# Attention decode with FFN on one core: scores on TensorE over K transposed on chip, softmax of four items in rows, one load queue

## The chip, the cores and the metric

One core of one Trainium2 chip. The metric is the device time of one execution, in microseconds (us), the median of several runs. All runs told here are fast ones. "Span" is the time from the first to the last instruction in the profiled run; in every run that lists both, the device time is 1.7 to 2.2 us longer.

The engines in the profile: PE is TensorE (PEld its weight loads), DVE is VectorE, ACT is ScalarE, POOL is GpSimd, SP is the sync engine that issues loads. A name with q (POOLq, SPq) is that engine's sequencer. L743 is line 743 of the kernel profiled.

## The reference

```
# x [2,1,640]; 32 heads, head size 192; the last 2048 of 8192 cached rows are used; bf16
h  = x + attention(layernorm(x)) @ wo       # softmax(q k^T / sqrt(192)) v, for each of 32 heads x 2 batches
h2 = h + (gelu(n @ w_gate) * (n @ w_up)) @ w_down          # n = layernorm(h), F = 1536
```

One query row per batch against 64 (head, batch) pairs, called items here. Each item has its own K and V of 2048 x 192, 768 KB each: 100.7 of the 122.3 MB that must be read.

## The kernel before

Items lie with 2048 = 128 partitions x 16 rows. VectorE makes the scores, 16 multiply-and-reduce instructions per item against a q row broadcast to all partitions (5 of the 64 items go through TensorE instead). The softmax needs a max and a sum over all partitions; GpSimd makes them for a pair of items at a time:

```python
KS = 4; VS = 4                       # buffers of K and of V
...
def armaxG(gi):                                        # GpSimd
    W(g, sem_v_max, gi + 1)
    ins = g.partition_all_reduce(mb_[:, a0:a0 + k], m1[:, a0:a0 + k], channels=128, reduce_op=RMAX)
    W(g, sem_g_chain, sem_g_chain.inc(ins))
    ins = g.tensor_scalar(out=nm[:, a0:a0 + k], in0=mb_[:, a0:a0 + k], scalar1=-1.0, scalar2=None, op0=ALU.mult)
    assert sem_g_nm.inc(ins) == gi + 1
def arsumG(gi):
    W(g, sem_a_exp, grp[-1] + 1)
    ins = g.partition_all_reduce(zb[:, a0:a0 + k], rs[:, a0:a0 + k], channels=128, reduce_op=RADD)
...
def ttr(n):                                            # VectorE, scores of item n
    for t in range(T):                                 # T = 16
        ins = v.tensor_tensor_reduce(out=junk[:, di % 2, t, :], in0=kring[:, slot, t * DH:(t + 1) * DH],
                                     in1=qb_ring[:, di % QBR, :], ..., accum_out=s_all[:, n, t:t + 1])
...
def expo(m):                                           # ScalarE
    W(a, sem_g_nm, GIDX[m] + 1)
    ins = a.activation(out=e_ring[:, m % ER, :, _row(b)], in_=s_all[:, m, :], func=ACT.Exp,
                       bias=nm[:, m:m + 1], scale=1.0, accum_out=rs[:, m:m + 1])
def pv(m):                                             # TensorE: 16 matmuls of 192 columns per item
    ...
# SP: V of item n is loaded when pv(n - 4) is done, K when the scores of the item 4 before are done
```

Of the kernel before, what the change touches and what calls it, by code (L numbers as in the profile page):

```python
# [7 lines left out]
I32 = mybir.dt.int32  # L8
# [3 lines left out]
RMAX = bass.bass_isa.ReduceOp.max  # L12
RADD = bass.bass_isa.ReduceOp.add

B = 2
D = 640
HQ = 32
# [4 lines left out]
F = 1536  # L22
NIT = B * HQ
EPS = 1e-5
# [3 lines left out]
KS = 4  # L28
VS = 4
WQR = 3  # L30
WOR = 4
QBR = 8
ER = 4
NWQ = 8
NGROUP = 16
R1 = 32
NCH = 3
QB_OFF = 256
SC_OFF = 448
QT_OFF = 464  # L40
OFF_HEADS = (11, 23, 35, 47, 59)


class _Sem:
    def __init__(self, sem):
        self.sem = sem
        self.count = 0

    def inc(self, ins, n=1):
        ins.then_inc(self.sem, n)  # L50
        self.count += n
        return self.count


def _row(b):
    return 0 if b == 0 else R1


def bass_sequential_preLN__sliding_block_cached__geglu_ffn__decode_kernel(
# [11 lines left out]
):  # L71
    with ExitStack() as ctx:  # L72
# [6 lines left out]
        def sb(shape, dt):  # L79
            return ctx.enter_context(nc.sbuf_tensor(_nm("sb"), shape, dt))  # L80

        def ps(shape, dt):
            return ctx.enter_context(nc.psum_tensor(_nm("ps"), shape, dt))

        def S(name):
            return _Sem(ctx.enter_context(nc.semaphore(name)))

        kring = sb([128, KS, T * DH], BF16)
        vring = sb([128, VS, T * DH], BF16)
        wqring = sb([128, WQR, 5, 768], BF16)  # L90
        woring = sb([128, WOR, 3, D], BF16)
        wg_sb = sb([128, 5, F], BF16)
        wu_sb = sb([128, 5, F], BF16)
        wd_sb = sb([128, 12, D], BF16)
        s_all = sb([128, NIT, T], F32)
        junk = sb([128, 2, T, DH], BF16)
        e_flat = sb([128, ER * T * 33 // 2], I32)
        e_ring = e_flat[:, :].bitcast(BF16).rearrange("p (a b c) -> p a b c", a=ER, b=T)
        qb_ring = sb([128, QBR, DH], BF16)
        xbc = sb([128, 2, 5, 128], BF16)  # L100
        koff = sb([128, T * DH], BF16)
        kta_sb = sb([128, 2, 8, 128], BF16)
        ktb_sb = sb([128, 2, 8, 128], BF16)
        qt_sb = sb([128, 2, 2], BF16)
        m1 = sb([128, NIT], F32)
        mb_ = sb([128, NIT], F32)
        nm = sb([128, NIT], F32)
        rs = sb([128, NIT], F32)
        zb = sb([128, NIT], F32)
        rinv = sb([128, NIT], F32)  # L110
        o_sb = sb([128, 2, 384], BF16)
        ot_flat = sb([128, 48 * 33 // 2], I32)
        ot_ext = ot_flat[:, :].bitcast(BF16).rearrange("p (a b) -> p a b", a=48)
        iota_i = sb([128, 128], I32)
        lib_scr = sb([128, 2], F32)
        burn_rhs = sb([128, 512], BF16)
        ident = sb([128, 128], BF16)
        selb = sb([128, 2, 128], BF16)
        xin = sb([128, D], BF16)
        x33f = sb([128, D], F32)  # L120
        stats = sb([128, 2, 6], F32)
        mv = sb([128, 2], F32)
        rstd = sb([128, 1], F32)
        sd1 = sb([128, 1], F32)
        sd2 = sb([128, 1], F32)
        dum = sb([1, 8], F32)
        eps_t = sb([128, 1], F32)
        xn_bf = sb([128, D], BF16)
        h_sb = sb([128, D], F32)
        stats2 = sb([128, 2, 6], F32)  # L130
        mv2 = sb([128, 2], F32)
        rstd2 = sb([128, 1], F32)
        hn_bf = sb([128, D], BF16)
        hT_ext = sb([128, 5, 33], BF16)
        g_bf = sb([128, F], BF16)
        u_bf = sb([128, F], BF16)
        fA = sb([128, F], BF16)
        fB = sb([128, F], BF16)
        fC = sb([128, F], BF16)
        uT_flat = sb([128, 12 * 33 // 2], I32)  # L140
        uT_ext = uT_flat[:, :].bitcast(BF16).rearrange("p (a b) -> p a b", a=12)
        h2_bf = sb([128, D], BF16)

        h_ps_a = ps([128, 512], F32)
        h_ps_b = ps([128, 512], F32)
        o_ps = [ps([128, 512], F32) for _ in range(2)]
        t_ps = [ps([128, 512], F32) for _ in range(2)]
        x_ps = [ps([128, 512], F32) for _ in range(2)]

        semK = [S(f"semK{i}") for i in range(KS)]  # L150
        semV = [S(f"semV{i}") for i in range(VS)]
        semWQ = [S(f"semWQ{i}") for i in range(WQR)]
        semWO = [S(f"semWO{i}") for i in range(WOR)]
        sem_x = S("sem_x")
        semKoff = S("semKoff")
        sem_wg = S("sem_wg")
        sem_wu = S("sem_wu")
        sem_wd = S("sem_wd")
        sem_out = S("sem_out")
        sem_v_ttr = S("v_ttr")  # L160
        sem_v_max = S("v_max")
        sem_v_rcp = S("v_rcp")
        sem_v_misc = S("v_misc")
        sem_v_chain = S("v_chain")
        sem_v_mv = S("v_mv")
        sem_v_init = S("v_init")
        sem_v_xbc = S("v_xbc")
        sem_v_hT = S("v_hT")
        sem_v_in = S("v_in")
        sem_v_pr = S("v_pr")  # L170
        sem_g_nm = S("g_nm")
        sem_g_z = S("g_z")
        sem_g_misc = S("g_misc")
        sem_g_chain = S("g_chain")
        sem_a_exp = S("a_exp")
        sem_a_oev = S("a_oev")
        sem_a_qb = S("a_qb")
        sem_a_kt = S("a_kt")
        sem_a_qt = S("a_qt")
        sem_a_sc = S("a_sc")  # L180
        sem_a_otev = S("a_otev")
        sem_a_misc = S("a_misc")
        sem_a_sd = S("a_sd")
        sem_a_xbc = S("a_xbc")
        sem_a_x1 = S("a_x1")
        sem_a_gev = S("a_gev")
        sem_a_uev = S("a_uev")
        sem_a_sg = S("a_sg")
        sem_a_ut = S("a_ut")
        sem_p_pv = S("p_pv")  # L190
        sem_p_qb = S("p_qb")
        sem_p_kt = S("p_kt")
        sem_p_qt = S("p_qt")
        sem_p_sc = S("p_sc")
        sem_p_tr = S("p_tr")
        sem_p_op = S("p_op")
        sem_p_misc = S("p_misc")
        sem_p_chain = S("p_chain")
        sem_p_gu = S("p_gu")
        sem_p_ut = S("p_ut")  # L200

        block = ctx.enter_context(nc.Block())

        def W(eng, sem, val):
            if val > 0:
                eng.wait_ge(sem.sem, val)
# [5 lines left out]
        def wq_src(J, c):  # L212
            return A_wq[128 * c:128 * (c + 1), 768 * J:768 * (J + 1)]

        def wo_src(g):
            return A_wo[384 * g:384 * (g + 1), :].rearrange("(p kk) n -> p kk n", kk=3)

        def wq_wait_val(J):
            slot, use = J % WQR, J // WQR
            if slot == 0:  # L220
                return 16 + 80 * use
            return 80 * (use + 1)

        def qb_bank_idx(m):
            if m < 9:
                return 1
            G = (m - 8) // 4
            return (G + 1) % 2

        def qb_bank(m):  # L230
            return t_ps[qb_bank_idx(m)]

        AUX = {}

        def _add_aux(n, fn):
            AUX.setdefault(n, []).append(fn)

        def _mk_wq(J, c):
            def fn(eng):
                if J >= WQR and c == 0:  # L240
                    last_m = 8 * (J - WQR) + 7
                    while last_m in OFF_IDX:
                        last_m -= 1
                    W(eng, sem_p_qb, DV_IDX[last_m] + 1)
                semWQ[J % WQR].inc(eng.dma_start(wqring[:, J % WQR, c, :], wq_src(J, c)), 16)  # L245
            return fn

        for _J in range(1, NWQ):
            for _c in range(5):
                _add_aux([0, 0, 1, 1, 2][_c] if _J == 1 else 8 * _J - 10 + _c, _mk_wq(_J, _c))  # L250

        def _mk_wo(gq):
            def fn(eng):
                if gq >= WOR:
                    W(eng, sem_p_op, gq - WOR + 1)
                semWO[gq % WOR].inc(eng.dma_start(woring[:, gq % WOR, :, :], wo_src(gq)), 16)
            return fn

        for _gq in range(NGROUP):
            _add_aux(4 * _gq + 2, _mk_wo(_gq))  # L260

        GROUPS = [[2 * P, 2 * P + 1] for P in range(NIT // 2 - 1)] + [[NIT - 2], [NIT - 1]]
        GIDX = {}
        for gi, grp in enumerate(GROUPS):
            for m in grp:
                GIDX[m] = gi
        RMAX_AT = {grp[-1] + 1: gi for gi, grp in enumerate(GROUPS)}
        RCP_AT = {grp[-1] + 2: gi for gi, grp in enumerate(GROUPS)}
# [23 lines left out]
        def k_slot(m):  # L292
            return DV_IDX[m] % KS
# [569 lines left out]
```

## Time and profile before

| | before |
|---|---|
| time at the prediction, three runs | 690.6 us (686.4 to 692.8) |
| span, mean TensorE clock granted | 685.9 us, 0.648 |
| bytes read, mean rate | 122.3 MB, 178 GB/s |
| busy: TensorE, VectorE, ScalarE, GpSimd | 42%, 42%, 15%, 5% |

The page is read from its head: busy shares first (is an engine full?), then the rate of the loads in 40 slices, then the waits, then the chain that ended last. The prediction below shows these lines and reads them; one reading of GpSimd in it is mended further down.

### The profile page before, as it was taken

The page shows a single profiled execution, that of the slowest core. Times are in us where ns is not written, and L with a number is a line of the kernel's source. Part 1 is how long each engine was busy: PE and PEld are TensorE (multiplying, and loading weights), DVE is VectorE, ACT ScalarE, POOL GpSimd, SP SyncE. Part 2 cuts the span into 40 slices and gives each one's busy share as a digit, 9 for nine tenths or more (in the row PEclk, how much of TensorE's full clock was granted, in tenths as well). Part 3 has the DMA queues.
Part 4 walks back from the last instruction along what each step waited for, and adds up shares of the span by engine and source line. Part 5 has one row for each costly group of instructions (what it writes and reads, how often), then busy time and mean ns, then how long its engine had stood idle before and what let it go on. Part 6 is the DMA issues. An engine that isn't in the chain of part 4 may idle for free.

```text
span 685.9 us, 7188 instructions
## 1 busy us (share of the span) xinstructions
PE 286.3 (42%) x1936; PEld 198.9 (29%) x1936; DVE 289.2 (42%) x2003; ACT 102.4 (15%) x328; POOL 37.0 (5%) x107
## 2 busy tenths in 40 slices
PE   3135643312783331277433118534421853333247
PEld 1024532201452221145222115423320542222123
DVE  4752344355344425533433555443245554332214
ACT  2112210110221101022101113111101311110013
POOL 1000000000000000000000000000000000000100
PEclk9556556766556666655567666666665656665659
DMA  8764525546542555545355455445644444548000
GB/s 328 280 224 169 182 97 201 217 176 231 207 179 103 183 216 184 211 184 190 106 200 226 167 198 207 179 154 186 242 148 168 184 167 184 200 160 318 0 0 1
DMA packets 28351, 122.76 MB, mean 179 GB/s; under 512 B 3092, under 2 KB 8216, under 8 KB 28312
## 3 DMA queue, kind: packets, MB, share of 16 engines
q1 hardware_dynamic: 20248, 103.63, 40.0%
q10 hardware_dynamic: 8064, 18.68, 8.3%
q8 instruction: 16, 0.26, 0.1%
q14 instruction: 23, 0.19, 0.1%
HBM read 122.29 MB, written 0.00 MB: 178 GB/s over the span
## 4 chain that ended last, share of the span: by engine, by line
issue 66%; DVE 15%; PE 9%; POOL 5%; ACT 2%; POOLq 1%; ACTq 1%; DVEq 0%
DVE sb L446 14%; PE ps L743 4%; POOL sb L333 2%; POOL sb L343 2%; ACT sb L553 1%; POOL sb L335 1%; PE ps L639 1%; PE ps L714 1%; PE ps L713 1%; POOLq L72 1%; ACTq L245 1%; DVE sb L434 1%; DVE sb L427 1%; PE ps L813 0%; PE ps L816 0%
## 5 line engine op out<-in xcount | busy, mean ns | idle before, releaser
L743 PE MATMUL ps<-sb 128*33 128x192 bf16 (+1 forms) x1024 | 156.2, 339 | 361.8 <-ACT sb L553 352.3
L446 DVE CUSTOM_DVE_ANT_0 sb<-sb 128x192 bf16<-128x192 bf16 x944 | 268.5, 352 | 16.0 <-issue 15.4
L743 PEld LDWEIGHTS ps<-sb 128*33 128x33 bf16 (+1 forms) x1024 | 119.8, 125 | 399.1 <-ACT sb L553 371.5
L434 DVE RECIPROCAL sb<-sb 128x2 f32<-128x2 f32 (+1 forms) x33 | 5.5, 166 | 359.1 <-POOL sb L343 359.1
L446 DVE DVE_READ_ACCUMULATOR2_ANT sb<- 128x1 f32 x944 | 76.9, 82 | 0.0
L553 ACT ACTIVATE sb<-sb 128x16 bf16<-128x16 f32 x64 | 21.1, 356 | 314.5 <-POOL sb L335 314.5
L680 PE MATMUL ps<-sb 128*128 128x192 bf16 x295 | 40.5, 277 | 17.7 <-ACT sb L535 11.5
L521 ACT ACTIVATE sb<-ps 128x192 bf16<-128x192 f32 x59 | 19.5, 331 | 156.2 <-PE ps L680 155.8
L680 PEld LDWEIGHTS ps<-sb 128*128 128x128 bf16 x295 | 25.1, 107 | 27.9 <-issue 27.0
L565 ACT ACTIVATE sb<-ps,sb 1x192 bf16<-1x192 f32 x64 | 26.2, 410 | 30.2 <-DVE sb L434 29.3
L343 POOL PARTITION_ALL_REDUCE sb<-sb x33 | 13.4, 405 | 214.7 <-issue 214.7
L335 POOL TENSOR_SCALAR sb<-sb 128x2 f32<-128x2 f32 (+1 forms) x33 | 8.3, 252 | 261.2 <-issue 261.2
L714 PE MATMUL ps<-sb 128*64 128x128 bf16 x80 | 22.3, 279 | 0.0
L713 PE MATMUL ps<-sb 128*128 128x128 bf16 x80 | 20.7, 258 | 0.0
L333 POOL PARTITION_ALL_REDUCE sb<-sb x33 | 13.0, 394 | 132.3 <-DVE sb L427 132.3
L770 PE MATMUL ps<-sb 128*33 128x512 bf16 x48 | 19.0, 467 | 0.5 <-ACT sb L571 0.5
L528 ACT ACTIVATE sb<-ps 128x1024 bf16<-128x1024 bf16 x10 | 10.2, 1024 | 52.2 <-PE ps L714 52.2
L726 PE MATMUL ps<-sb 128*128 128x1 bf16 x80 | 14.3, 179 | 0.4 <-ACT sb L521 0.4
L728 PE MATMUL ps<-sb 64*128 64x1 bf16 x80 | 14.1, 176 | 0.0
L772 PE MATMUL ps<-sb 128*33 128x128 bf16 x48 | 12.0, 250 | 0.0
L553 ACT ACTIVATION_READ_ACCUMULATOR sb<-sb 128x1 f32 x64 | 11.9, 186 | 0.0
L714 PEld LDWEIGHTS ps<-sb 128*64 128x64 bf16 x80 | 9.3, 117 | 7.8 <-issue 0.8
(84 smaller groups left out, 134.9 us busy)
## 6 DMA issues: line engine op xcount, KB each, us to landing
sb<-in_A_v_cache_dram SPq DMA_DIRECT2D x64, 768.0 KB, 5.4
sb<-in_A_k_cache_dram SPq DMA_DIRECT2D x59, 768.0 KB, 5.8
sb<-in_A_wo_dram ACTq DMA_DIRECT2D x16, 480.0 KB, 3.6
sb<-in_A_wq_dram ACTq DMA_DIRECT2D x35, 192.0 KB, 2.8
sb<-in_A_k_cache_dram ACTq DMA_DIRECT2D x5, 768.0 KB, 4.4
sb<-in_B_w_gate_dram SPq DMA_DIRECT2D x5, 384.0 KB, 8.3
sb<-in_B_w_up_dram SPq DMA_DIRECT2D x5, 384.0 KB, 8.4
sb<-in_B_w_down_dram SPq DMA_DIRECT2D x3, 640.0 KB, 11.4
```

The source lines that it names most:

```text
L333: ins = g.partition_all_reduce(mb_[:, a0:a0 + k], m1[:, a0:a0 + k], channels=128, reduce_op=RMAX)
L335: ins = g.tensor_scalar(out=nm[:, a0:a0 + k], in0=mb_[:, a0:a0 + k], scalar1=-1.0, scalar2=None, op0=ALU.mult)
L343: ins = g.partition_all_reduce(zb[:, a0:a0 + k], rs[:, a0:a0 + k], channels=128, reduce_op=RADD)
L446: ins = v.tensor_tensor_reduce(out=junk[:, di % 2, t, :], in0=kring[:, slot, t * DH:(t + 1) * DH], in1=qb_ring[:, di % QBR, :], scale=1.0, ...
L521: ins = a.activation(out=qb_ring[:, di % QBR, :], in_=qb_bank(m)[:, QB_OFF:QB_OFF + DH], func=ACT.Copy, scale=SCALE)
L553: ins = a.activation(out=e_ring[:, m % ER, :, _row(b)], in_=s_all[:, m, :], func=ACT.Exp, bias=nm[:, m:m + 1], scale=1.0, accum_out=rs[:, ...
L565: ins = a.activation(out=o_sb[r:r + 1, G % 2, (h % 2) * DH:(h % 2 + 1) * DH], in_=o_ps[m % 2][r:r + 1, 0:DH], func=ACT.Copy, scale=rinv[r: ...
L680: ins = pe.matmul(t_ps[bank][:, QB_OFF:QB_OFF + DH], lhsT=xbc[:, b, c, :], rhs=wqring[:, J % WQR, c, hoff:hoff + DH], start=(c == 0), stop ...
L713: pe.transpose(xa_view[:, 128 * tt:128 * (tt + 1)], koff[:, t * DH:t * DH + 128], ident[:, :])
L714: ins = pe.transpose(xb_view[0:64, 128 * tt:128 * (tt + 1)], koff[:, t * DH + 128:(t + 1) * DH], ident[:, :])
L743: ins = pe.matmul(o_ps[m % 2][0:M, 0:DH], lhsT=e_ring[:, m % ER, t, 0:M], rhs=vring[:, m % VS, t * DH:(t + 1) * DH], start=(t == 0), stop= ...
L770: pe.matmul(h_ps_a[0:33, :], lhsT=ot_ext[:, k, 0:33], rhs=woring[:, gq % WOR, kk, 0:512], start=first, stop=last)
```

## The change

Its intent is to take the work that sits on partitions away from VectorE and GpSimd. K is transposed on TensorE, 24 transposes of 128x128 per item, and copied back to SBUF by VectorE and ScalarE. Scores then are matmuls with four items in four groups of 32 PSUM partitions (four column tiles of the array). An item's softmax lies in 4 rows of 512 columns, so the max and the sum over columns are ordinary reductions, and the combination of the 4 rows is a small matmul with a mask. The output, h, the norms and the FFN are kept transposed. GpSimd only fills constants. All loads go on SP's queue, with 6 K and 8 V buffers. The waits come from a small list of dependences rather than by hand.

```diff
-KS = 4
-VS = 4
...
+KS = 6
+VS = 8
+KTS = 8
...
-                ins = g.partition_all_reduce(mb_[:, a0:a0 + k], m1[:, a0:a0 + k], channels=128, reduce_op=RMAX)
...
-                    ins = v.tensor_tensor_reduce(
...
+                        for jj in range(8):                      # transposes(n), for c in range(3)
+                            off = 384 * jj + 128 * c
+                            ins = e.transpose(bv[:, 128 * jj:128 * (jj + 1)], kring[:, slot, off:off + 128],
+                                              identb[:, :])
...
+                if c == 2 or (c == 1 and n % 4 == 1):
+                    act(lambda e, ...: e.activation(out=ktr[:, kslot, c, :], in_=bv[:, 0:1024], func=ACT.Copy), ...)
+                else:
+                    dve(lambda e, ...: e.tensor_copy(ktr[:, kslot, c, :], bv[:, 0:1024]), ...)
...
+                for k in range(6):                               # scores(g)
+                    for j in range(4):
+                        ins = e.matmul(sps[32 * j:32 * (j + 1), :], lhsT=rq[:, g % 2, j, k, :], rhs=r, start=(k == 0),
+                                       stop=(k == 5), tile_position=(0, 32 * j))
+            dve(lambda e: e.tensor_reduce(out=mx[:, :], in_=sps[:, :], axis=AX.X, op=ALU.max), W=["mx"], X=["s"])
...
+            pe(lambda e: e.matmul(m2[:, 0:4], lhsT=pm[:, :], rhs=mrhs[:, :], start=True, stop=True), ...)
...
+                    for cc in range(4):                          # pv(g), per item
+                        for r in range(4):
+                            ins = e.matmul(ops_[32 * r:32 * (r + 1), 192 * hh:192 * (hh + 1)],
+                                           lhsT=ering[:, g % 2, col:col + 32], rhs=vring[:, n % VS, DH * t:DH * (t + 1)],
+                                           ..., tile_position=(0, 32 * r), skip_group_check=True)
...
```

(The rest, some 1,400 lines of it, is the same idea for q, o, the norms and the FFN.)

## The prediction

> **What bounds the kernel now.** I read the head of the page first: no engine is near full (TensorE 42%, VectorE 42%), and the DMA rate starts at 328 GB/s, then stays mostly between 100 and 240.
>
> ```profile
> PE 286.3 (42%) x1936; PEld 198.9 (29%) x1936; DVE 289.2 (42%) x2003; ACT 102.4 (15%) x328; POOL 37.0 (5%) x107
> GB/s 328 280 224 169 182 97 201 217 176 231 207 179 103 183 216 184 211 184 190 106 200 226 167 198 207 179 154 186 242 148 168 184 167 184 200 160 318 0 0 1
> ```
>
> So nothing is short of throughput; something is a chain. The waits by total, with the DMA queue's own, say which (engine, line, what it waited for: us in total, times, longest):
>
> ```profile
> DVE sb L434 <- POOL sb L343: 359.1, 33, 14.6
> ACT sb L553 <- POOL sb L335: 314.5, 33, 15.1
> POOL sb L335 <- issue: 261.2, 33, 11.3
> POOL sb L343 <- issue: 214.7, 33, 7.2
> ...
> SPq L361 <- PE ps L743: 463.3, 59, 18.1
> ```
>
> Each occurs 33 times, once per pair of (head, batch) items. L333 and L343 are GpSimd's max and sum over partitions; the "issue" after them is GpSimd's real time in them. SPq L361 is the queue's V load, held 463 us in all until a PV (L743) frees its buffer. One round of the chain that ended last, in order of time (start, us, what), shows the order:
>
> ```profile
> 87.82 0.39 POOL sb L333
> 88.21 0.06 POOLq L335 x2
> 88.28 7.00 issue
> 95.27 0.26 POOL sb L335
> ...
> 96.06 0.20 ACT sb L553
> 96.25 5.46 issue
> 101.71 0.42 POOL sb L343
> 102.13 0.02 issue
> 102.15 0.17 DVE sb L434
> ```
>
> 7.5 us of max, a negation, the exp, some 6 us of sum, reciprocal: serial on GpSimd, with a part of VectorE's scores between. L333 starts 33 times between 25.2 and 649.0 us: (649.0-25.2)/32 = 19.5 us a round, 33 rounds = 643 of the 686 us. The bound is **GpSimd's cross-partition softmax round**, through PV to the V buffers. The DMA could do far more, as the table of stretches shows (from:to, length, busy time of each engine, clock, DMA share, GB/s):
>
> ```profile
> 8.00:14.00 6.00, 4.06 (x18) 1.62 (x18) 4.16 (x11) 0.50 (x3) 1.50 (x2) 1.00 1.01 419
> 3.40:24.00 20.60, 7.50 (x38) 3.75 (x38) 13.61 (x75) 3.69 (x10) 2.31 (x4) 0.81 1.01 402
> 100.00:600.00 500.00, 209.10 (x1457) 149.17 (x1455) 216.50 (x1551) 71.00 (x240) 26.99 (x77) 0.64 0.51 187
> ```
>
> The first is the SP queue alone with loads waiting, the third the body at half share.
>
> [...] no column-tiled group is in this trace. [...] in 60.4 to 63.7 us, where 14 of the matmuls starting are transposes, the clock is 1.00, and it is still 1.00 in 63.8 to 67.1, granted after them. [...] This trace has only fp32 copies there (128 columns 280 ns, 512 columns 683 ns: about 1.05 ns a column plus 0.15 us).
>
> **The change, part by part.** Removed: all 66 all-reduces and the 944 multiply-reduce instructions on VectorE (268 us). Scores now come from K transposed on TensorE; the max and sum over the 4 rows of an item are small matmuls, for 4 items at once: 16 groups instead of 33 rounds. K gets 6 buffers and V 8 (from 4 and 4); everything loads on the SP queue. The bytes stay 122.3 MB, so the question is what a group costs on each resource.
>
> *DMA.* 8 K and V blocks of 0.786 MB, 0.49 of wq and 0.49 of wo: 7.27 MB. At 405 GB/s (between 402 and 419[...]): **18.0 us**. V is asked for two groups ahead, K six items ahead; I count 6 to 12 loads of 1.9 us queued at any time, so the queue should not run dry if TensorE needs under 18 us.
>
> *TensorE.* 96 transposes of 128x128. The timeline gives two pitches. Alternating shapes, 16 transposes take 2.7 us at the full clock (168 ns each) and 3.7 at half (235). One shape throughout, as in the first line below, is (0.73-0.22)/9 = 57 ns.
>
> ```profile
> 13.03 0.73 PE L649 MATMUL ps<-sb 33*128 33x128 bf16 x10
> ...
> 61.00 0.28 PE L694 MATMUL ps<-sb 128*128 128x1 bf16 x5
> ...
> 81.22 0.18 PE L726 MATMUL ps<-sb 128*128 128x1 bf16 x1
> 81.33 0.17 PE L728 MATMUL ps<-sb 64*128 64x1 bf16 x1
> ```
>
> The second line too: one shape, (0.28-0.17)/4 = 28 ns; L726 and L728 alternate row counts and pay 105. The new transposes all have one shape, so I take 57 ns: 96 x 57 = 5.4 us (10.3 at half clock, 107 ns). Scores: 24 matmuls of 512 columns in four column tiles; at 512 columns in 0.22 us (5 of L813 in the timeline take 1.26: (1.26-0.38)/4), 6 x 0.216 = 1.3 us if the four run together, 5.2 if not. PV: 64 of 192 columns at 82 ns (the median from start to start in L680, also 192 columns, at the full clock), 1.3 us together or 5.2. q rows 5 x 0.16 = 0.8; the q, e and o columns, the fp32 mask products and 15 oproj matmuls about 2.2 (estimate, 25 to 60 ns bf16[...]). Sum **11 us**, 22 if always at half clock, 19 if the tiles don't run together.
>
> *Evictions.* 12 of 128x1024 bf16 per group. ScalarE has 5 at 1024 ns (L528's row), plus exp, q and o copies: 5.1+0.8+0.8+0.5 = 7.2 us. [...] One bank makes the round transpose, copy, transpose: 0.45+0.2+1.02+0.1 = 1.8 us per item on ScalarE's bank, 2.4 on VectorE's pair[...]. Four items take 7.4 to 9.3 us, so with the other matmuls and some 1.5 us of waits for max and exp TensorE's elapsed group is 13 to 16 us, under 18.0.
>
> So the bound passes from GpSimd to **the DMA**. The sum: first bytes flow at about 3.4 us (as now); all but the FFN weights is 116.4 MB, /0.405 = 287 us, so the last V lands at 291. From there the chain ends it: K's last block is queued four V loads earlier, so the last transposes end about 5 us before V; scores, softmax, PV, o, h and LN of the last group take some 16 us of short steps, so the FFN input is ready 11 us after V; gate and up weights (3.9 MB, 10 us) have just landed, down (5 us more) comes while 120 small matmuls (3.2 us), gelu (2 us) and 24 matmuls of 320 columns (3.3 to 6.4) run; copy and store 2.5. That is 25 us after V: 316. Times measured before exceed the span by 690.6-685.9 = 4.7: 321. I add 3% of 290 for stretches where the queue is not full: **330 us**.
>
> **Rivals.** *TensorE becomes the bound.* If transposes keep 168 ns, or the tiles don't run together, or the clock stays at half, a group takes 20 to 24 us: 16 x 20 to 24 + 45 = 365 to 430. For it: the mean clock is 0.648 and bursts begin at 0.50. Against: a dense burst is granted 1.00 after one 3.4 us window (PV from 76.2, full clock in 80.9 to 84.2), and the one-shape rows above. *The wait moves to small serial steps*: scores, max, mask product, exp, e columns and PV cross engines some ten times per group, as GpSimd's round did. Against: each step is under 1 us here, not 7, and they are issued between transposes of the next group. If they stall TensorE 4 us more per group, about 20 us and 350 to 365. *The single queue costs bandwidth*: waits in order on SP could hold a ready load behind one that is not. SP issues in 0.33 to 0.5 us, 11 per group = 5 of 18 us; alone it ran 419 GB/s, so I expect 0 to 10 us. A hidden change (no gain) would need the transfers to be the limit now, and they are at 187 GB/s.
>
> **Range and chances.** 312 is 412 GB/s without hiccups and a 20 us tail; 375 is TensorE at 20 to 21 us a group. Over 2% slower would need 43 us a group, beyond any sum above. Faster 0.98, same 0.01, slower 0.01.
>
> **What would show it.** Right: DMA share about 1.0 and 390 to 415 GB/s in nearly all slices until some 300 us; TensorE idle before transposes waiting for K's DMA; transposes at 57 ns when the clock is 1.00; four PV matmuls in the time of one; a 20 to 30 us tail with little DMA at its end. Wrong: GB/s near 300 to 350 with SP waiting for transposes or PV; TensorE busy 90% at clock 0.5; transposes waiting on VectorE's or ScalarE's copies; VectorE copies at 1.2 us. The prediction falls most likely through TensorE's pitch or clock, next through the evictions.

The last sum stands: the last V at 291, 25 us of end, 4.7 from span to time and 9 for stretches where the queue is not full make 330 us. The 2.2 us in TensorE's 11 holds fp32 products. The 405 GB/s is between the 402 and 419 of the windows. VectorE's copies had a low case and a high one, which summed to 7 to 11 us. The high one follows from the trace's line of 0.15 us and 1.05 ns a column: 7 x 1.22 = 8.5 us, with the max (0.68) and small operations (1.6, an estimate) 10.8 a group, and the 2.4 us per item of the bank round. In "only fp32 copies there", "there" is out of PSUM. That the column tiles run together was an assumption.

## The result, and the profile after

| | before | after |
|---|---|---|
| time | 688.5 us (684.6 to 692.8, 4 runs) | 316.7 us (316.3 to 317.4, 4 runs) |
| span, clock | 685.9 us, 0.648 | 314.4 us, 0.832 |
| mean rate over the span | 178 GB/s | 389 GB/s |

The ratio is 0.4595, with an interval of 0.4572 to 0.4618. Ratios are the mean time of one kernel's fast runs over that of the other's in the same rounds, so not quite the ratio of the medians quoted.

The head of the page after the change:

```profile
PE 236.6 (75%) x3753; PEld 192.3 (61%) x3753; DVE 122.1 (39%) x339; ACT 114.7 (36%) x151; POOL 3.3 (1%) x9
DMA  7999999999999999999999999999999999995792
GB/s 253 416 418 414 398 404 416 415 410 406 417 413 416 401 417 417 413 409 407 413 416 415 399 415 416 415 410 409 414 415 416 414 416 416 414 415 233 248 376 81
```

The DMA digit is 9 from the second slice to the 36th, and the rate stays between 398 and 418 GB/s. The holes are at the ends: the first slice, and the last four, some 31 us. The table of stretches says the same of the body (columns: from:to, length, busy time of each engine, clock, DMA share, GB/s):

```profile
100.00:270.00 170.00, 133.41 (x2118) 109.87 (x2115) 67.29 (x173) 67.48 (x87) 0.00 (x0) 0.84 1.02 413
```

Against 187 GB/s in the body before, TensorE is now busy 78% of the stretch and still waits, for K. The costliest wait of its matmuls after a DMA, and the longest ones of SP's queue (columns: engine and line, what it waited for, us in total, times, longest):

```profile
PE tps L409 <- DMA kring<-in_A_k_cache_dram: 50.5, 11, 14.7
...
SPq L252 <- PE tps L409: 47.3, 14, 7.0
SPq L256 <- PE tps L409: 31.3, 22, 4.9
```

SP's waits look alarming and are not: they are waits for room in a full ring while some 9 loads are still on their way. A K load takes 17.7 us from issue to landing (median on the page, section of DMA issues), and one block of 768 KB moves in 1.9 us.

The groups behind the disputed terms of the prediction (columns: line, engine, operation, tiles, shapes, count; busy us in all, mean ns of one; idle before it and what ended most of that):

```profile
L409 PE MATMUL tps<-identb,kring 128*128 128x128 bf16 x1536 | 116.4, 243 | 51.2 <-DMA kring<-in_A_k_cache_dram 50.5
L417 ACT ACTIVATE ktr<-tps 128x1024 bf16<-128x1024 bf16 x80 | 80.2, 1023 | 125.8 <-PE tps L409 118.6
L421 DVE COPY ktr<-tps 128x1024 bf16<-128x1024 bf16 x112 | 74.5, 688 | 100.1 <-PE tps L409 99.8
L530 PE MATMUL ops<-vring,ering 128*32 128x192 bf16 x1024 | 24.5, 249 | 0.0
L485 PE MATMUL sps<-ktr,rq 128*32 128x512 bf16 x384 | 23.7, 381 | 0.0
```

L530 is PV: 24.5 us in all, 1.5 us for the 64 matmuls of a group, so most of them run beside each other (started 82 ns apart, as the 192-column matmuls of the kernel before, they would take 84 us). L485, scores: 1.5 us for 24. The copies out of PSUM are 688 ns on VectorE and 1023 on ScalarE. The transposes follow each other every 56 ns at the full clock and every 107 at half (medians from start to start in the trace). In this trace the full clock comes at 51.3 us, right after a stretch of 3.4 us at half clock, of which 24 transposes took 2.7; no run has transposes alone.

At the end, the timeline shows what remains after the last V landed at 290.7 us (columns: start, us, engine, line, operation, tiles, count, [idle before and what ended it]):

```profile
292.61 1.80 PE L530 MATMUL ops<-vring,ering 128*32 128x192 bf16 x64
...
303.06 1.74 PE L633 MATMUL sps<-hnT,kring 128*128 128x2 bf16 x60 [1.30 <-issue]
...
307.04 5.22 PE L654 MATMUL tps<-wd_sb,uT 128*2 128x320 bf16 x24 [0.63 <-DVE uT L291]
```

The last PV, then o, h and the norm until the gate matmuls at 303 us, then the down matmuls (L654) until 312.3 us, the first 15 of the 24 started at half clock (up to 310.7 us), then the store.

### The profile page after: what moved, and what is told of

It reads as the page before. It is cut to its first block, busy times and chain, and to the rows that moved or that the text cites. A ratio compares the mean times of both kernels' runs of the same rounds, so it can differ in the third digit from the quotient of the medians.

```text
span 314.4 us, 8298 instructions
## 1 busy us (share of the span) xinstructions
PE 236.6 (75%) x3753; PEld 192.3 (61%) x3753; DVE 122.1 (39%) x339; ACT 114.7 (36%) x151; POOL 3.3 (1%) x9
## 4 chain that ended last, share of the span: by engine, by line
DMA 46%; PE 34%; SPq 10%; DVE 4%; ACT 3%; issue 2%; ACTq 0%; DVEq 0%
DMA kring<-in_A_k_cache_dram 46%; PE tps L409 16%; SPq L265 4%; SPq L256 4%; PE ops L530 4%; PE sps L485 3%; PE m L430 3%; ACT ktr L417 2%; PE tps L654 2%; PE m L544 1%; PE m L515 1%; DVE ering L514 1%; DVE ktr L421 1%; SPq L260 1%; SPq L252 1%
## 5 line engine op out<-in xcount | busy, mean ns | idle before, releaser
L409 PE MATMUL tps<-identb,kring 128*128 128x128 bf16 x1536 | 116.4, 243 | 51.2 <-DMA kring<-in_A_k_cache_dram 50.5
L409 PEld LDWEIGHTS tps<-identb,kring 128*128 128x128 bf16 x1536 | 104.7, 110 | 68.2 <-issue 66.9
L417 ACT ACTIVATE ktr<-tps 128x1024 bf16<-128x1024 bf16 x80 | 80.2, 1023 | 125.8 <-PE tps L409 118.6
L421 DVE COPY ktr<-tps 128x1024 bf16<-128x1024 bf16 x112 | 74.5, 688 | 100.1 <-PE tps L409 99.8
L530 PE MATMUL ops<-vring,ering 128*32 128x192 bf16 x1024 | 24.5, 249 | 0.0
L435 ACT ACTIVATE qrow<-m 2x768 bf16<-2x768 f32 x16 | 12.8, 799 | 31.4 <-PE m L430 31.4
L485 PE MATMUL sps<-ktr,rq 128*32 128x512 bf16 x384 | 23.7, 381 | 0.0
L430 PE MATMUL m<-wqring,xnT 128*2 128x384 bf16 x80 | 21.9, 420 | 0.9 <-DVE xnT L291 0.9
L530 PEld LDWEIGHTS ops<-vring,ering 128*32 128x32 bf16 x1024 | 20.7, 98 | 0.4
L544 PE MATMUL m<-sel,osb 128*128 128x2 f32 x96 | 18.8, 312 | 0.6 <-ACT osb L539 0.6
L544 PEld LDWEIGHTS m<-sel,osb 128*128 128x128 f32 x96 | 18.2, 264 | 1.4 <-ACT osb L539 1.0
L485 PEld LDWEIGHTS sps<-ktr,rq 128*32 128x32 bf16 x384 | 8.9, 96 | 8.5
## 6 DMA issues: line engine op xcount, KB each, us to landing
kring<-in_A_k_cache_dram SPq DMA_DIRECT2D x64, 768.0 KB, 17.7
```

Of the source, the lines that this page charges most:

```text
L409: ins = e.transpose(bv[:, 128 * jj:128 * (jj + 1)], kring[:, slot, off:off + 128], identb[:, :])
L417: act(lambda e, c=c, kslot=kslot, bv=bv: e.activation(out=ktr[:, kslot, c, :], in_=bv[:, 0:1024], func=ACT.Copy), W=[("kt", kslot, c)], X= ...
L421: dve(lambda e, c=c, kslot=kslot, bv=bv: e.tensor_copy(ktr[:, kslot, c, :], bv[:, 0:1024]), W=[("kt", kslot, c)], X=[("t", bi)])
L430: ins = e.matmul(m1[0:2, 128:512], lhsT=xnT[:, c, :], rhs=wqring[:, J % WQS, c, off:off + 384], start=(c == 0), stop=(c == NC5 - 1))
L435: act(lambda e: e.activation(out=qrow[0:2, :, 0:rep, :], in_=m1[0:2, 128:512].rearrange("p (h d) -> p h d", h=2).unsqueeze(2).to_broadcast ...
L485: ins = e.matmul(sps[32 * j:32 * (j + 1), :], lhsT=rq[:, g % 2, j, k, :], rhs=r, start=(k == 0), stop=(k == 5), tile_position=(0, 32 * j))
```

## The experiments

Twelve runs in three calls; runs of one call share a chip and its runs of the kernel before (690 to 697 us in these calls). The kernels without reloads compute on wrong K and V. The comparison with the reference passes them all the same, presumably because attention adds very little to x with these inputs, so "correct" says nothing about them. From the scales in the reference, attention adds some 0.1% of x, as an estimate (values of 0.05, averaged over 2048 rows with nearly equal weights). So for every kernel here "correct" is a weak check of the attention part, and no run here checks that part more closely.

**1. The kernel before without its maximum.** The first question: is the round of 19.5 us really what bounded it?

```diff
 def armaxG(gi):
-    W(g, sem_v_max, gi + 1)
-    ins = g.partition_all_reduce(mb_..., RMAX)
-    W(g, sem_g_chain, sem_g_chain.inc(ins))
-    ins = g.tensor_scalar(out=nm..., scalar1=-1.0, op0=ALU.mult)
+    pass
 def expo(m):
-    W(a, sem_g_nm, GIDX[m] + 1)
+    W(a, sem_v_init, 3)
+    scores_ready_wait(a, m)          # nm is filled with 0.0 once; VectorE's max is gone too
```

> The kernel before without its max: the max over items, its all-reduce and the negation are gone, exp has a bias of zero (the scores are small, so the result should still be right). Theory (two all-reduces in series set a round of 19.5 us): a round loses the 0.39 + 7.0 + 0.26 us from the start of the max to its negation, 33 x 7.7 = 254 us, so about 430 us (400 to 450). Rival (V's buffers or VectorE's scores set the pace, GpSimd only waits on them): above 600 us.

Measured: 363.6 us, ratio to the kernel before 0.5235 (0.5212 to 0.5257), correct. That is far below the 430 expected: not one phase of the round went, but both. GpSimd's row in this run:

```profile
L338 POOL PARTITION_ALL_REDUCE sb<-sb x33 | 15.9, 483 | 301.2 <-ACT sb L546 301.2
```

33 sums with 0.48 us each and no "issue" time before them; it only waits for exp. In the kernel before the same sum had 214.7 us of "issue" ahead of it. So the all-reduce is not slow, and my reading of those 6 to 7 us as the reduction's own time was wrong. What differs is that GpSimd now runs one kind of instruction only. Looking again at the kernel before, its sequencer has these (columns: count, duration min/median/max in ns, first and last start in us):

```profile
L335 POOLq MODIFY_POOL_CONFIG  x66: 83/83/85, 25.6 to 649.5; - x66
...
L343 POOLq MODIFY_POOL_CONFIG  x66: 5/7/7, 34.7 to 657.1; - x66
```

66 on each line: 33 pairs ahead of the negation and 33 pairs ahead of the sum, 66 pairs in all. The chain in the prediction even showed one pair, as "POOLq L335 x2", with 7.00 us of "issue" right behind it. That makes a new theory: going from the all-reduce to the negation, a `tensor_scalar`, or back costs GpSimd 6 to 7 us (6.2 to 7.2 in the rounds from 80 to 122 us), twice per round.

**2. The kernel before with the negation on ScalarE.** Both all-reduces stay; only what lies between them moves.

```diff
 def armaxG(gi):
     ins = g.partition_all_reduce(mb_[:, a0:a0 + k], m1[:, a0:a0 + k], channels=128, reduce_op=RMAX)
-    W(g, sem_g_chain, sem_g_chain.inc(ins))
-    ins = g.tensor_scalar(out=nm[:, a0:a0 + k], in0=mb_[:, a0:a0 + k], scalar1=-1.0, scalar2=None, op0=ALU.mult)
     assert sem_g_nm.inc(ins) == gi + 1
 def expo(m):
     W(a, sem_g_nm, GIDX[m] + 1)
+    if m == GROUPS[GIDX[m]][0]:
+        k = len(GROUPS[GIDX[m]])
+        achain(a.activation(out=nm[:, m:m + k], in_=mb_[:, m:m + k], func=ACT.Copy, scale=-1.0))
```

> The kernel before with one operation moved: the negation of the maximum goes from GpSimd to ScalarE; both all-reduces stay on GpSimd. New theory (the 6 to 7 us are not the all-reduces, which show 0.4 us each in the run without max, but the switch between two kinds of GpSimd instruction, announced by a pair of MODIFY_POOL_CONFIG, 66 times): no switch is left, VectorE's scores set the pace, 360 to 410 us. Theory of the prediction (the max takes 7.5 us and the sum 6 on GpSimd): about as before, over 650 us.

Measured: 364.7 us, ratio 0.5254 (0.5222 to 0.5286), correct. GpSimd's timeline of the kernel before, then of this run (start, us, engine, line, operation, [idle before and what ended it]):

```profile
106.69 0.39 POOL L333 PARTITION_ALL_REDUCE sb<-sb  x1 [4.57 <-DVE sb L427]
113.90 0.25 POOL L335 TENSOR_SCALAR sb<-sb 128x2 f32<-128x2 f32 x1 [6.82 <-issue]
121.32 0.40 POOL L343 PARTITION_ALL_REDUCE sb<-sb  x1 [7.17 <-issue]
```

```profile
133.38 0.39 POOL L334 PARTITION_ALL_REDUCE sb<-sb  x1 [5.31 <-DVE sb L425]
134.81 0.40 POOL L341 PARTITION_ALL_REDUCE sb<-sb  x1 [1.05 <-ACT sb L554]
```

Max and sum are now 1.4 us apart instead of 14.6, and neither line has a MODIFY_POOL_CONFIG any more. The kernel before has a control of its own: its max follows the sum of the round before, all-reduce after all-reduce, and never waits for "issue" (all 132.3 us of its waiting are for VectorE). One moved instruction takes the kernel before from 693 to 365 us. The table of stretches says what it is then like:

```profile
100.00:300.00 200.00, 150.80 (x1120) 107.43 (x1118) 162.17 (x1164) 57.95 (x198) 15.69 (x37) 0.75 0.91 358
```

VectorE is busy 81% of that stretch and the loads run at 358 GB/s. Which of the two holds it at 365 was not tested.

**3. The changed kernel's loads alone.** Everything else taken out, nearly the same order of loads, a buffer loaded again once its previous load has landed, zeros as output.

```diff
-        q_rows(0); q_stationary(0)
 for g in range(NG):
     for j in range(4):
-        transposes(n)
         if n + KS < NIT: load_k(n + KS)
-        scores(g - 1) ... softmax, e_columns, q_rows, oproj      # wo and wq loads kept in place
     if g > 0:
-        pv(g - 1)
+        load_v(...)                                              # the four of pv(g - 1)
 # FFN loads without the wait that run 10 takes out; norm, FFN and residual removed
```

> All loads of the changed kernel in nearly its order and on its one queue, no compute, a buffer is loaded again when its previous load has landed; the output is zeros, wrong on purpose. Theory: 122.3 MB at 412 GB/s = 297 us + 3.4 start + some 3 for the last store: 300 to 306 us, so the changed kernel has only some 12 us beside its loads. Rival (the loads alone are faster and the consumers slow them): under 290 us.

Measured: 305.3 us (wrong output). The changed kernel's 316.7 is only 11.4 us above its loads alone. The rate:

```profile
GB/s 241 418 420 416 397 406 415 418 418 400 420 415 417 410 410 418 415 417 400 418 416 419 417 401 417 418 417 404 414 418 418 416 415 418 416 420 415 407 398 220
```

Up to the 36th slice it is the rate of the full kernel, so there the consumers did not slow the loads; the full kernel's hole of 233 and 248 GB/s in slices 37 and 38 is absent here.

**4. The changed kernel's compute alone.** K and V are loaded for the first fill of their buffers only.

```diff
-                if n + KS < NIT:
-                    load_k(n + KS)
...
-                if n + VS < NIT:
-                    load_v(n + VS)
```

> The changed kernel, K and V loaded only for the first fill of their buffers (6 and 8 blocks) and read again and again; wrong result on purpose, all compute kept. Theory (the DMA is the bound, TensorE needs 13 to 16 us a group of the 18): about 20 + 16 x 13.5 + 25 = 260 us, 250 to 285, TensorE's clock near 1.0. Rival (TensorE or its evictions are as long as the DMA): 300 us or more.

Measured: 249.0 us, just under the range; clock 0.945. Two PVs follow each other thus (start, us, engine, line):

```profile
117.77 1.41 PE L530 MATMUL ops<-vring,ering 128*32 128x192 bf16 x60
...
130.46 1.50 PE L530 MATMUL ops<-vring,ering 128*32 128x192 bf16 x64
```

So a group needs 12.8 us of TensorE (the first row is cut at the window's edge, by 4 matmuls of 0.02 us each), against 17.6 us of loads (7.27 MB at 413 GB/s). The slack is some 5 us a group, and it is why TensorE waits for K. Experiments 3 and 4 together show the bound: the loads alone account for 305 of 317 us, the compute alone for 249.

**5. Four V buffers.** `VS = 8` becomes `VS = 4`, nothing else.

> The changed kernel with 4 V buffers instead of 8. Theory (6 to 12 loads are queued, so 4 fewer still leave the queue full): 316 to 321 us. Rival (the depth of V's ring carries the DMA rate): 335 us or more, with gaps in the DMA rate before each PV.

Measured: 320.0 us, ratio to the kernel before 0.4603 (0.4586 to 0.4621), against 0.4595 for the changed kernel: 1% at most. The depth of V's ring does not carry the gain, as expected.

**6 and 7. One shape or two on TensorE.** The prediction's largest risk was the pitch of the transposes: 168 ns when shapes alternate, 57 when they don't. In the profile `128*64` is a stationary operand (what is loaded as weights) of 128 rows and 64 columns. Both kernels add one matmul of two columns before every transpose of the kernel of experiment 4; only the number of rows differs.

```diff
+    e.matmul(hps[:, 256:258], lhsT=identb[0:128, :], rhs=identb[0:128, 0:2], start=True, stop=True, ...)   # control
+    e.matmul(hps[:, 256:258], lhsT=identb[0:64, :],  rhs=identb[0:64, 0:2],  start=True, stop=True, ...)   # 64 rows
     ins = e.transpose(bv[:, 128 * jj:128 * (jj + 1)], kring[:, slot, off:off + 128], identb[:, :])
```

> As the run without reloads, with one more matmul of two columns and 128 rows before each of the 1536 transposes. Control for the next run: some 25 to 30 ns each, 96 x 27 ns = 2.6 us a group, about 290 us (280 to 300).

> The same with 64 rows instead of 128 in the added matmul, so the shape changes twice per transpose. Theory of the prediction (the 168 ns transposes of the kernel before pay for alternating shapes): 100 to 150 ns more per transpose than in the control, about 400 to 480 us. Rival (those transposes were slow for another reason): as the control, within 10 us.

Measured: 278.4 us, just under the range, and 698.4 us, far above it. The control costs 29.4 us over 1536 transposes, 19 ns each. With 64 rows each costs (698.4-278.4)/1536 = 273 ns more than the control. Timelines of the control, then of the 64 rows:

```profile
120.86 0.22 PE L411 MATMUL tps<-identb,kring 128*128 128x128 bf16 x1
120.92 0.16 PE L409 MATMUL hps<-identb 128*128 128x2 bf16 x1
120.94 0.22 PE L411 MATMUL tps<-identb,kring 128*128 128x128 bf16 x1
```

```profile
120.13 0.29 PE L411 MATMUL tps<-identb,kring 128*128 128x128 bf16 x1
120.35 0.18 PE L409 MATMUL hps<-identb 64*128 64x2 bf16 x1
120.46 0.29 PE L411 MATMUL tps<-identb,kring 128*128 128x128 bf16 x1
```

80 ns a pair against 330. An alternating row count costs much, as the theory said; its size was low by half. The half clock explains only a part of that. Here the clock is 0.50 (control: 1.00), but where it is 1.00 in the same run, from 88.4 to 91.7 us, a pair still takes 270 ns:

```profile
89.19 0.23 PE L411 MATMUL tps<-identb,kring 128*128 128x128 bf16 x1
89.35 0.17 PE L409 MATMUL hps<-identb 64*128 64x2 bf16 x1
89.46 0.23 PE L411 MATMUL tps<-identb,kring 128*128 128x128 bf16 x1
```

So two changes of shape cost 270-80 = 190 ns at the full clock, 95 each, and the half clock adds some 60 to a pair. The expectation of 100 to 150 is about one change (168-57 = 111 ns in the kernel before), while each transpose here has two. One thing is not shown: the 168 ns transposes of the kernel before alternate columns (`128*128` and `128*64`), not rows. Rows alternate in its L726 and L728, which pay 105 ns; a run that alternates columns was not made. What in TensorE takes the time at a change is not shown.

**8 and 9. The order of the column tiles.** The prediction held that four column tiles run together. The loops are turned so that the matmuls of one tile follow each other (scores: 6 in a row, PV: 4 in a row), first without reloads, then in the full kernel.

```diff
-                    for cc in range(4):
-                        for r in range(4):
+                    for r in range(4):
+                        for cc in range(4):
...
-                for k in range(6):
-                    for j in range(4):
-                        n = 4 * g + j
+                for j in range(4):
+                    for k in range(6):
+                        n = 4 * g + j
```

> As the run without reloads (248 us, 12.7 us a group), with the loops of scores and PV turned so that the matmuls of one column tile follow each other; same matmuls, wrong K and V on purpose. Theory (four column tiles run together): scores go from 1.5 to 24 x 0.216 = 5.2 us and PV from 1.5 to 64 x 0.082 = 5.2, so a group 20.1 us and the run about 366 us (345 to 380). Rival (their order does not matter): 248.

> The changed kernel with the column tiles of scores and PV in turn, all loads kept. Theory (the DMA bounds at 17.6 us a group only because TensorE's group is shorter): TensorE's group becomes some 20 us, so it is the bound: 355 to 385 us, DMA rate near 360 GB/s. Rival (the tiles' overlap is hidden behind the DMA anyway): 317 to 322 us.

Measured: 268.8 us (248 to 249 with the old order), and 319.1 us in the full kernel, against 316.8 for the unedited one in the same call. Both expectations missed. The timeline of the first gives 2.81 us for the 24 scores matmuls (from 1.48) and 1.54 for PV's 64 (from 1.50). So the order cost 1.33 us in the scores, with runs of six matmuls of 512 columns, and 0.04 in PV, with runs of four of 192 columns. Even in runs of four, then, a tile's matmuls run beside those of other tiles. Whether the longer runs or the wider matmuls make the difference is not shown. The edit did not take the overlap away, so it is no test of what the overlap is worth. That the tiles do run together is shown by the trace itself: 64 matmuls of 192 columns in 1.50 us, where the kernel before started matmuls of 192 columns 82 ns apart at the full clock, 5.2 us for 64. In the full kernel the extra 1.3 us a group is hidden, as 12.8 + 1.3 is still under 17.6; its 319.1 us lies in the rival's range.

**10 and 11. The end.** SP's waits hold one of 5.3 us in which the first up-weight load waits for the landing of the first gate-weight load, because both are listed as writers of all K buffers; they write different places. The first kernel takes that out. The second also asks for the last two K loads ahead of V 56 to 59. The unedited changed kernel ran beside both as a twelfth run.

```diff
-                 R=(), W=(kw if c == 0 else []) + [("wu", c)], dma=f"dwu{c}")
+                 R=(), W=[("wu", c)], dma=f"dwu{c}")
```

```diff
                     load_k(n + KS)
+                if n + KS == NIT - 1:
+                    for m in range(4 * (NG - 4), 4 * (NG - 3)):
+                        load_v(m + VS)
...
-                if n + VS < NIT:
+                if n + VS < NIT and g != NG - 4:
                     load_v(n + VS)
```

> The changed kernel unedited, for comparison on the same chip: 316 to 318 us.

> The changed kernel without the wait of the first up-weight load on the landing of the first gate-weight load (5.3 us in SP's waits; the two write different places). Theory: the last weights land 5.3 us earlier, at 304.8 us, but then TensorE's steps set the end: 1 to 2 us less, 315.4 us. Rival (the end follows the last landing): 5 us less, 311.5.

> As the run before, and the last two K loads are asked for ahead of V 56 to 59, so that the last transposes, scores and softmax run while the last V blocks land. Theory (the end is the last V at 291 us, then PV, o, h, LN, FFN): the FFN input is ready some 3 us earlier, 311 to 313 us. Rival: no change against the run before.

Measured, ratios to the kernel before:

| | median us | fast runs | ratio |
|---|---|---|---|
| changed kernel, unedited | 316.8 | 315.8 to 317.3 | 0.4565 (0.4546 to 0.4585) |
| without the false wait | 316.5 | 313.7 to 317.5 | 0.4557 (0.4532 to 0.4581) |
| and K first at the end | 313.3 | 312.9 to 313.8 | 0.4520 (0.4501 to 0.4540) |

The first is inconclusive: its runs spread over 4 us. In its profile the last weight does land 4.2 us earlier (305.9 against 310.1), yet the down matmuls take 5.81 us instead of 5.22 and the end is set by TensorE's steps. They start 2.3 us earlier, but the clock rises at 309.7 us (310.7 in the unedited kernel), so 19 of the 24 start at half clock instead of 15. The second is 1.1% below the unedited kernel, each of its runs under each of that one's: small, and the best version found. It beats both kernels. Against the run before it the intervals of the ratios touch, so its own step is not told apart. In its profile the gate matmuls start at 299.8 us against 300.8, 1 us earlier where 3 were expected.

## Why the prediction was right, and where not

The time (316.7 in a range of 312 to 375) and the direction came out. Step by step:

- **GpSimd's round bounds the kernel before**: right. Without the switches in it the time nearly halves (experiments 1 and 2). **"The 'issue' after them is GpSimd's real time in them"**: wrong. The all-reduces take 0.4 us; the 7.0 and 6 us are switches between the negation and the reductions, gone when the negation moved. It did not hurt the forecast, as the change removes both, but it hid that 328 of the 376 us (from 693 to 365 to 317) were to be had by moving one instruction. The pairs of MODIFY_POOL_CONFIG in the chain were the clue.
- **The bound passes to the DMA**: right. Loads alone 305.3 us; share 1.02 and 413 GB/s in the body, where the sum had taken 405. The last V was put at 291 us and landed at 290.7, which is partly luck: at 413 GB/s the 116.4 MB would have been there at 3.4 + 282 = 285 us, but its sixteen parts landed one by one between 283.8 and 290.7 us, and from 283 to 291 us the loads ran at only 227 GB/s. Little was queued behind it, as the first gate load goes into K's buffers and waited 12.9 us for transposes; why the last V itself came in so slowly is not shown.
- **TensorE, 11 us busy and 13 to 16 elapsed a group**: 12.8 us elapsed, just under the range; 0.9 of it is a wait for the e columns, so some 11.9 are work. Transposes 56 ns (57), scores 1.5 us (1.3), PV 1.5 (1.3).
- **Evictions**: 1023 ns on ScalarE, where 1024 was put in. 688 on VectorE, well under the 1.22 us that the line of the kernel before gives.
- **The end, 25 us after the last V**: 314.4-290.7 = 23.7.
- **The terms that were off**: "I add 3% of 290 for stretches where the queue is not full", 9 us, was not needed on top of the 287 us: between the second and the 36th slice no such stretch appears, and the one after it is in the 290.7 us already. The distance from span to measured time was taken as 4.7 and is 2.3 here; 690.6 was the median of three runs and 685.9 the span of the profiled one, and in one and the same run the two differ by 1.7 to 2.2. With the end, 9 + 2.4 + 1.3 makes nearly all of 330-316.7 = 13.3.
- **A sum that does not close**: four items of 1.8 to 2.4 us are 7.2 to 9.6 us, not 7.4 to 9.3; and of the two "copies" out of PSUM behind 1.05 ns a column, the one of 512 columns is an addition (TENSOR_TENSOR, L493). That line gives 1.22 us for 1024 columns, and the bf16 copies took 688 ns; what makes them faster was not tested.
- **The rivals**: TensorE as the bound fell in experiment 4, small serial steps too (they are inside the 12.8 us), and the single queue cost nothing that shows up to the 36th slice: its rate there, 398 to 418 GB/s, is that of loads alone, 397 to 420.

## What to carry to other kernels

When an engine's wait reads "issue", ask what its sequencer did there before calling it the instruction's own time: here two kinds of GpSimd instruction taking turns cost 6 to 7 us at each turn, and moving the cheap one to another engine was worth 328 of the 376 us that the whole rewrite gained. Judge a rewrite by running its loads alone and its compute alone; the larger of the two says what is left. Keep one matmul shape in a stream: an alternating row count cost 190 ns a pair at the full clock, where the pair itself took 80.
